# Chunks 10 and 11 of the FFN move to the seven-product second layer, and the order of the whole program is written anew

## The chip, the cores and the metric

The kernel runs on one core of a Trainium2 chip. The metric is the device time of one execution in microseconds (us). Engines: PE is TensorE (matmuls; PEld is its weight load), DVE is VectorE, ACT is ScalarE, POOL is GpSimd, SP is SyncE, which here issues nearly all DMAs. Each engine runs its own instructions strictly in the order in which the program writes them.

## The reference, cut to what matters

```python
# q, k, v: (8, 8, 576, 64); w_ch1: (512, 2048); w_ch2: (2048, 512)
scores = scale * np.matmul(q, k.transpose(0, 1, 3, 2))
mask = (rel >= 0) & (rel < 64)                 # each query sees 64 keys
scores = np.where(mask, scores, -1000000000.0)
scores = scores - np.max(scores, axis=-1, keepdims=True)
attn = np.exp(scores)
attn = attn / (np.sum(attn, axis=-1, keepdims=True) + 1e-09)
x = np.matmul(attn, v)                         # -> (8, 576, 512)
u = x + np.real(np.fft.fft(np.fft.fft(x, axis=1), axis=2))
un = (u - mu) / np.sqrt(var + 1e-06)           # norm over the last axis
out = u + np.maximum(un @ w_ch1, 0.0) @ w_ch2
```

## The kernel before

**Work and tiles.** The 8 x 576 = 4,608 tokens are 36 tiles of 128 tokens, 9 for each pair of batches. Nearly every product is done in fp16 parts: an operand is split into a high and a low half, and a product is three matmuls (`PASSES`: high x high, high x low, low x high).

**Attention, tile by tile.** q, k and v are loaded (L538), from tile 11 on split into halves and turned by transposing DMAs (L593). The PE makes the scores (L662), the DVE masks them and takes the maximum (L677), ACT does the exponential (L685), ACT, POOL and DVE split the result into `flex` (L506, L510, L516), a transposing DMA for each half tile writes it to `pt` (L715), and the PE multiplies by the values, `pa<-ve,pt` and `pa<-va,pt` (L739). The DVE normalises (L758), and another transposing DMA turns the result (L865) for the FFT (L1023, L1061 on the PE). For tiles from 14 on the attention result goes out to DRAM and comes back later (L791, L1228). After a batch's FFT each tile is gathered, normalised and turned by one more transposing DMA, `room<-up` (L1221); `room` then holds the input of the FFN.

**FFN, chunk by chunk.** The tokens form 18 chunks (0 to 17) of 256. The first layer is the same in all: 16 hidden blocks f, each 12 matmuls of 128x128 weights by 256 columns into `ph` (L1419, or L1573 in the newer form). The second layer has two forms.

- `ffn(c)`, for chunks below `SEVEN`: for each f six matmuls of 512 columns, `po<-ws,hh` (L1400); the hidden values are made by ACT (L1428) and DVE (L1431), 512 columns at a time.
- `ffn7(c)`, for chunks from `SEVEN` on: hidden blocks j and j+8 are taken together as a 2x2 block product, done with seven products of sums in place of eight. For each of 8 j there are 7 x 3 = 21 matmuls of 256 columns (L1548). The sums of the hidden values are made by DVE or POOL (L1589), then split (L506, L510, L1597). The sums of the weights, the same for all chunks, are made once by `weight_sums(j)` on the DVE (tiles `td`, L1493 to L1521) and are kept in buffers that attention uses until its end: `flex`, `qbd`, `kst`, `va`, `ve`.

**What sets the order.** The program first lists some 3,000 operations with what each reads and writes. A table of their numbers, `ORDER`, then says in which order they are issued, and a set, `SECOND`, which operations go to their second choice of engine. The FFN chunks are spread under the attention of later tiles, so that the PE has matmuls while DVE, ACT, POOL and the DMAs prepare the next tile. Before the first FFN work, `warm` matmuls (L1759) stand in gaps of the PE. The lines around the change:

```python
            for c in range(max(PLAIN, made), min(SEVEN, ready)):
                ffn(c)
    ...
    for j in range(HALF):
        weight_sums(j, 4000 + 10 * j)
    for c in range(SEVEN, NCH):
        plan.slack = FSLACK
        ffn7(c)
    ...
        for o, gap in zip(plan.follow(ORDER, SECOND), plan.gaps):
```

Of the kernel before, what the change touches and what calls it, by code (L numbers as in the profile page):

```python
# [58 lines left out]
SEVEN = 12  # L59
# [339 lines left out]
def attn_fft_ffn_kernel(ctx: ExitStack, tc: tile.TileContext, q, k, v, w1, w2, gidx, dft_d, dft_s, mask, out):  # L399
# [1311 lines left out]
    for T in range(NTT):  # L1711
# [6 lines left out]
        if n in (4, 8):  # L1718
            base += FFT_AT + (FFT1 if T == 8 else 0)
            fft(2 * pb + n // 8, base)  # L1720
            for i, m in enumerate(range(0, 4) if n == 4 else range(4, 9)):
                args = NT * pb + m, base + NORM_AT + i + (EARLY if T == 4 and i > 1 else 0)
                if args[0] // 2 >= SEVEN + 4:
                    behind.setdefault(args[0] // 2, []).append(args)
# [66 lines left out]
```

## Time and profile before

| what | value |
|---|---|
| median of 3 runs | 944.51 us (944.35 to 948.38) |
| profiled execution, whole | 945.16 us |
| its span in the trace | 943.4 us |
| PE busy in the span | 924.2 us (98%) |
| DVE, ACT, POOL busy | 705.3 us (75%), 435.1 us (46%), 441.5 us (47%) |
| granted PE clock | 1.000 over the whole span |
| last PE instruction of attention | about 654 us |

The span is what the profiler saw between first and last instruction; the 1.8 us between 943.4 and 945.16 lie outside it. Busy times of different engines overlap. A PE that is busy all the time is bound by what it streams; then a DVE that idles costs nothing.

### The profile page before, as it was taken

To read this page: it belongs to the slowest core of one execution; us is meant where nothing else is said; L and a number is where in the kernel's file an instruction comes from. 1 tells how busy PE (TensorE), PEld (TensorE's weight loads), DVE (VectorE), ACT (ScalarE), POOL (GpSimd) and SP (SyncE) were. 2 spreads that over 40 slices of the span, in tenths; PEclk is the share of its full clock that TensorE was granted. 3 is DMA by queue.
4 is the path that set the end of the run, shared out by engine and by line. 5 is a ranking of instruction groups with operands and counts; after the bars stand their busy time and mean duration, and the time that the engine had idled before them with its cause. 6 is when DMAs were issued, how large, how long until landed. Compare 5 with 4: busy or idle time off the path is not lost.

```text
span 943.4 us, 24809 instructions
## 1 busy us (share of the span) xinstructions
PE 924.2 (98%) x9717; PEld 703.2 (75%) x9717; DVE 705.3 (75%) x1982; ACT 435.1 (46%) x979; POOL 441.5 (47%) x823
## 2 busy tenths in 40 slices
PE   7799999999999999999999999999999999999998
PEld 6677777666766676666766676667779998888887
DVE  5898998887767866677658757888898965675664
ACT  6875777834555424445443543444334442422111
POOL 2653464744744555465746544655601454124012
PEclk9999999999999999999999999999999999999999
DMA  9997447999689969879979788785402032210100
GB/s 231 239 263 202 133 144 147 167 173 169 136 193 163 198 122 167 185 152 207 197 168 190 150 162 169 163 147 108 137 12 57 24 96 65 68 35 13 57 24 23
DMA packets 300230, 128.69 MB, mean 136 GB/s; under 512 B 277768, under 2 KB 278152, under 8 KB 300112
## 3 DMA queue, kind: packets, MB, share of 16 engines
q1 hardware_dynamic: 297248, 118.06, 59.6%
q0 software_dynamic: 2720, 8.92, 3.3%
q8 instruction: 76, 1.25, 0.6%
q14 instruction: 42, 0.34, 0.1%
q10 hardware_dynamic: 144, 0.13, 0.0%
HBM read 60.76 MB, written 19.94 MB: 86 GB/s over the span
## 4 chain that ended last, share of the span: by engine, by line
PE 83%; DMA 5%; DVE 4%; POOL 3%; SPq 2%; issue 2%; ACT 1%; POOLq 0%; DVEq 0%; ACTq 0%
PE ph L1419 22%; PE po L1400 22%; PE ph L1573 13%; PE po L1548 11%; PE pz L1061 3%; PE pg L1023 3%; PE pa L739 3%; PE psc L662 2%; DMA kn<-in_k 1%; POOL flex L516 1%; DMA ve<-va 1%; DMA qn<-in_q 1%; DMA pt<-flex 1%; SPq L1277 1%; PE py L850 1%
## 5 line engine op out<-in xcount | busy, mean ns | idle before, releaser
L1400 PE MATMUL po<-ws,hh 128*128 128x512 f16 (+1 forms) x1116 | 284.5, 391 | 0.5 <-issue 0.2
L1419 PE MATMUL ph<-room,ws 128*128 128x256 f16 x2112 | 256.1, 273 | 1.8 <-DVE hh L1431 1.8
L1419 PEld LDWEIGHTS <-ws 128*128 128x128 f16 x2112 | 205.3, 98 | 54.1 <-issue 2.8
L1400 PEld LDWEIGHTS <-hh 128*128 128x128 f16 x1056 | 101.1, 98 | 90.0 <-DVE hh L1431 0.7
L1573 PE MATMUL ph<-room,ws 128*128 128x256 f16 x1152 | 136.2, 273 | 0.0
L1573 PEld LDWEIGHTS <-ws 128*128 128x128 f16 x1152 | 112.6, 98 | 13.6
L1428 ACT ACTIVATE hh<-ph 128x512 f16<-128x512 f32 x88 | 52.3, 594 | 120.8 <-PE ph L1419 99.8
L685 ACT ACTIVATE pr<-pr,nm 128x128 f32<-128x128 f32 x288 | 91.2, 393 | 31.5 <-DVE nm L677 31.4
L1431 DVE SCALAR_TENSOR_TENSOR hh<-ph,hh 128x512 f16<-128x512 f32 x88 | 60.4, 686 | 36.6 <-ACT hh L1428 36.5
L1135 POOL DMA_INDIRECT mt<-md,gix x34 | 42.0, 1235 | 96.7 <-DVE mv L1163 81.5
L677 DVE CUSTOM_DVE_ANT_0 pr<-psc,mskb 128x128 f32<-128x128 f32 x288 | 65.0, 287 | 25.9 <-PE psc L662 19.7
L1584 ACT ACTIVATE hx<-ph 128x512 f32<-128x512 f32 x47 | 27.8, 595 | 113.3 <-PE ph L1573 103.7
L1589 DVE TENSOR_TENSOR hx<-hx 128x128 f32<-128x128 f32 x164 | 45.1, 318 | 37.8 <-ACT hx L1584 36.2
L1548 PEld LDWEIGHTS <-hh 128*128 128x128 f16 x658 | 64.4, 98 | 7.6
L1597 POOL TENSOR_TENSOR hl<-hx,hh 128x256 f16<-128x256 f32 (+1 forms) x40 | 28.0, 730 | 77.3 <-DVE hh L510 53.7
L516 POOL TENSOR_TENSOR up<-un,up 128x128 f16<-128x128 f32 x84 | 40.9, 516 | 46.3 <-ACT up L506 38.8
L516 POOL TENSOR_TENSOR flex<-pr,flex 128x128 f16<-128x128 f32 x92 | 42.5, 494 | 36.2 <-ACT flex L506 18.2
L1548 PE MATMUL po<-ws,hh 128*128 128x256 f16 x282 | 51.2, 273 | 0.0
L1597 DVE TENSOR_TENSOR hl<-hx,hh 128x896 f16<-128x896 f32 x37 | 40.4, 1097 | 7.8 <-ACT hh L506 6.5
L752 POOL TENSOR_TENSOR rc<-rc,mone 128x4 f32<-128x4 f32 x29 | 32.5, 1129 | 26.6 <-DVE rc L747 16.8
L739 PE MATMUL pa<-ve,pt 128*64 128x65 f16 (+1 forms) x776 | 37.0, 203 | 2.5 <-ACT ve L506 1.8
L1548 PE MATMUL po<-ws,hl 128*128 128x256 f16 x141 | 38.4, 273 | 0.0
(244 smaller groups left out, 1718.6 us busy)
## 6 DMA issues: line engine op xcount, KB each, us to landing
room<-in_moe_w_ch SPq DMA_DIRECT2D x20, 512.0 KB
flex<-in_moe_w_ch SPq DMA_DIRECT2D x12, 512.0 KB
ve<-va SPq DMA_DIRECT2D x47, 130.0 KB
flex<-in_v SPq DMA_DIRECT2D x22, 256.0 KB
xs<-xu SPq DMA_DIRECT2D x22, 256.0 KB
xv<-xs SPq DMA_DIRECT2D x22, 256.0 KB
out<-xv SPq DMA_DIRECT2D x21, 256.0 KB
md<-mp SPq DMA_DIRECT2D x24, 192.0 KB
```

The costliest lines, as they stand in the source:

```text
L516: eng.tensor_tensor(out=out[:, k : k + w], in0=in0[:, k : k + w], in1=in1[:, k : k + w], op=al)
L677: nc.vector.tensor_tensor_reduce(out=t["pr", g][:, hp], in0=t["ps", g][:, hp], in1=mskb[:, m : m + P], scale=-0.125, scalar=3.0e38, op0=AL ...
L685: nc.scalar.activation(pr, pr, AF.Exp, bias=t["nm", g][:, hp : hp + 1], scale=-1.0)
L739: nc.tensor.matmul(pa[sl, hp], pt[:, sl], v_, start=(x == 0), stop=(x == len(mm) - 1))
L1400: nc.tensor.matmul(t["po"][i], l_, r_, start=(f == 0 and x == 0), stop=(f == NKF - 1 and x == len(mm) - 1))
L1419: nc.tensor.matmul(ph, l_, r_, start=(x == 0), stop=(x == len(mm) - 1))
L1428: nc.scalar.activation(t["hh", j][:, 0], ph, AF.Relu)
L1431: nc.vector.scalar_tensor_tensor(out=hh[:, 1], in0=ph, scalar=0.0, in1=hh[:, 0], op0=ALU.max, op1=ALU.subtract)
L1548: nc.tensor.matmul(t["po", bk][:, x], t["h", j][a][:, slot], right(n, j, b_), start=(j == 0 and k == 0 and n in opens), stop=(j == seven - ...
L1573: nc.tensor.matmul(ph, l_, r_, start=(x == 0), stop=(x == len(mm) - 1))
L1589: eng.tensor_tensor(out=x[:, o], in0=x[:, p0], in1=x[:, p1], op=al)
L1597: eng.tensor_tensor(out=lo[:, a:b_], in0=x[:, a + 1 : b_ + 1], in1=hi[:, a:b_], op=ALU.subtract)
```

## The change

`SEVEN` goes from 12 to 10: chunks 10 and 11 leave `ffn` for `ffn7`. The seven-product form then has eight chunks, 10 to 17. The two-layer chunks 0 to 9 alone are left for the time before and during attention. `ORDER` and `SECOND` are written anew for the whole program. Nothing else in the code differs.

```diff
-SEVEN = 12
+SEVEN = 10
 AWAY = 14
 
 ORDER = [int(i) for i in """
-1 115 0 9 7 116 3 15 118 119 120 145 121 124 144 129 16 149 125 130 173 126 131 147 150 117 127 148 17 132 21 18 176 153
...
+8 0 9 3 7 116 14 115 15 120 121 144 145 118 119 124 125 126 127 129 130 149 150 117 123 16 146 173 147 148 131 122 128
...
```

Counted over the program on the PE: 192 fewer matmuls of 512 columns at L1400 and 336 more of 256 columns at L1548; 384 matmuls of the first layer change their line from L1419 to L1573; 48 `warm` matmuls in place of 45. On the other engines: the four-part sums of L1589 go from 164 to 196 on the DVE and from 24 to 56 on POOL; L1597 from 37 to 47 on the DVE and from 40 to 64 on POOL; L1431 on the DVE from 88 to 72.

Fewer chunks now lie under attention. Between the scores of tile 20 and those of tile 32 the PE had 81 groups of L1419 (12 matmuls) and 81 of L1400 (6 matmuls); now 61 and 62. The transfers that load q, k and v or transpose (1,024 packets of at most 256 bytes each) between these two places are 109 before and 103 now. Between the scores of tile 26 and of tile 32 the groups go from 39 and 39 to 30 and 31, and the transfers from 55 to 56.

First place, the PE at the second half of tile 31's product with the values (`pa<-ve,pt` and `pa<-va,pt`). `pt_0` and `pt_1` are the two buffers that the turned halves take in turn. Before, 36 matmuls of L1400, 83 of L1419 and 24 of L1023 stand between the tile's scores and this place:

```order
L1419 LDWEIGHTS ws
L1419 MATMUL ph_4_9579<-room,ws 128x256
L1419 LDWEIGHTS ws
L1419 MATMUL ph_4_9579<-room,ws 128x256
L739 LDWEIGHTS pt_0_9516
L739 MATMUL pa_0_9602<-ve_85,pt_0_9516 64x65
L739 LDWEIGHTS pt_0_9516
L739 MATMUL pa_0_9602<-va_83,pt_0_9516 64x65
```

and of the kernel changed, where 18 matmuls of L1400, 36 of L1419, 12 of L1061 and 48 of L739 stand between:

```order
L1400 LDWEIGHTS hh_6_8717
L1400 MATMUL po_1_8148<-ws,hh_6_8717 128x512
L1400 LDWEIGHTS hh_6_8717
L1400 MATMUL po_1_8148<-ws,hh_6_8717 128x512
L739 LDWEIGHTS pt_1_8926
L739 MATMUL pa_1_8996<-ve_85,pt_1_8926 64x65
L739 LDWEIGHTS pt_1_8926
L739 MATMUL pa_1_8996<-va_83,pt_1_8926 64x65
```

The same product now stands closer behind the scores of its own tile.

Second place, the queue of SP around the transposes that make these `pt` tiles (`room` is the FFN's input, `qbd`, `kst`, `va`, `ve` are parts of q, k and v, `md` goes to DRAM, `py` is a turned result for the FFT). Before:

```order
L1221 DMA_TRANSPOSE room<-up_9447 128x8x128
L715 DMA_TRANSPOSE pt_1_9489<-flex 128x8x128
L715 DMA_TRANSPOSE pt_0_9516<-flex 128x8x128
L538 DMA qbd_79<-in_q 128x8x64
L624 DMA ve_85<-va_83 64x520
L538 DMA flex<-in_v 128x8x64
L1086 DMA md_7577<-mp_2_9184 96x512
L865 DMA_TRANSPOSE py_9654<-yp_9542 128x8x128
```

and of the kernel changed:

```order
L593 DMA_TRANSPOSE qbd_78<-flex 128x8x128
L593 DMA_TRANSPOSE kst<-flex 128x8x128
L715 DMA_TRANSPOSE pt_1_8926<-flex 128x8x128
L1086 DMA md_7626<-mp_1_8899 96x512
L1221 DMA_TRANSPOSE room<-up_8870 128x8x128
L538 DMA flex<-in_v 128x8x64
L1228 DMA xv_8974<-xs_7128 128x512
L715 DMA_TRANSPOSE pt_0_9023<-flex 128x8x128
```

The transpose of `pt_1` now stands right behind the two that turn the next tile's q and k.

Third place, the DVE at the first weight sums (`td`). `ws` holds the weights. Before, with the work on tile 34 around them:

```order
L1194 TENSOR_SCALAR un_10182<-xv_9949,rs_10198,nb_10364 128x512
L1431 SCALAR_TENSOR_TENSOR hh_1_10224<-ph_1_10133,hh_1_10224 128x512
L516 TENSOR_TENSOR yT_9166<-yT_9166 128x4x96
L1493 TENSOR_TENSOR td_0_10400<-ws 128x512
L1493 TENSOR_TENSOR td_0_10400<-td_0_10400,ws 128x512 x2
L1500 TENSOR_TENSOR td_1_10401<-ws,td_0_10400 128x256
L1501 TENSOR_TENSOR td_1_10401<-td_1_10401,ws 128x256
L1502 TENSOR_TENSOR td_1_10401<-ws,td_1_10401 128x256
```

and of the kernel changed:

```order
L1431 SCALAR_TENSOR_TENSOR hh_6_9810<-ph_6_9699,hh_6_9810 128x512
L955 SCALAR_TENSOR_TENSOR h_6_9917<-h_6_9692,yT_8587 128x388
L1493 TENSOR_TENSOR td_0_9919<-ws 128x512
L1493 TENSOR_TENSOR td_0_9919<-td_0_9919,ws 128x512 x2
L1500 TENSOR_TENSOR td_1_9920<-ws,td_0_9919 128x256
L1501 TENSOR_TENSOR td_1_9920<-td_1_9920,ws 128x256
L1502 TENSOR_TENSOR td_1_9920<-ws,td_1_9920 128x256
L1503 TENSOR_TENSOR td_1_9920<-td_1_9920,ws 128x256
```

From the first of these rows to the last `td` row the DVE has 246 instructions before and 220 in the kernel changed. The whole of attention moves likewise: the last tile's scores stood on the PE inside chunk 10, and stand now at the start of chunk 9.

## Rows read from the trace of the kernel before

**Rows 1.** The page: busy time by engine, and slices of the span.

```profile
PE 924.2 (98%) x9717; PEld 703.2 (75%) x9717; DVE 705.3 (75%) x1982; ACT 435.1 (46%) x979; POOL 441.5 (47%) x823
...
PEclk9999999999999999999999999999999999999999
DMA  9997447999689969879979788785402032210100
```

**Rows 2.** Windows: busy time by engine in four stretches.

```profile
core 0: us, PE busy (x) PEld busy (x) DVE busy (x) ACT busy (x) POOL busy (x), PEclk, DMA share, GB/s
0.00:23.60 23.60, 18.64 (x244) 14.53 (x244) 11.99 (x64) 14.86 (x37) 7.00 (x23) 1.00 0.97 231
23.60:60.00 36.40, 30.66 (x407) 24.54 (x406) 33.10 (x118) 28.98 (x76) 26.04 (x41) 1.00 0.99 242
190.00:640.00 450.00, 445.83 (x5282) 315.27 (x5281) 327.31 (x1021) 201.62 (x497) 246.95 (x494) 1.00 0.87 169
790.00:840.00 50.00, 50.00 (x460) 44.81 (x459) 35.29 (x87) 18.31 (x29) 15.37 (x26) 1.00 0.23 59
```

**Rows 3.** The chain of waits, 396 to 425 and 800 to 815 us.

```profile
398.08 1.29 PE po L1400 x6
399.37 1.31 PE ph L1419 x12
...
803.51 2.29 PE po L1548 x21
805.81 1.31 PE ph L1573 x12
```

**Rows 4.** Groups of instructions by line, shapes apart (busy us, mean ns).

```profile
L1400 PE MATMUL po<-ws,hh 128*128 128x512 f16 x1056 | 256.4, 379 | 0.5 <-issue 0.2 <-DVE hh L1431 0.2
...
L1548 PEld LDWEIGHTS <-hh 128*128 128x128 f16 x658 | 64.4, 98 | 7.6
L1431 DVE SCALAR_TENSOR_TENSOR hh<-ph,hh 128x512 f16<-128x512 f32 x88 | 60.4, 686 | 36.6 <-ACT hh L1428 36.5
...
L1589 DVE TENSOR_TENSOR hx<-hx 128x128 f32<-128x128 f32 x164 | 45.1, 318 | 37.8 <-ACT hx L1584 36.2
```

**Rows 5.** What the PE waited for, 150 to 943 us (total, times, longest).

```profile
PE ph L1419 <- DVE hh L1431: 1.8, 3, 1.3
PE psc L662 <- issue: 1.3, 3, 0.6
PE pa L739 <- DMA ve<-va: 0.5, 1, 0.5
```

**Rows 6.** DMA packets, 195 to 245, 275 to 325 and 240 to 640 us.

```profile
DMA packets 30779, 9.16 MB, mean 183 GB/s; under 512 B 30068, under 2 KB 30068, under 8 KB 30772
...
DMA packets 29114, 9.35 MB, mean 187 GB/s; under 512 B 28191, under 2 KB 28191, under 8 KB 29108
...
DMA packets 183852, 67.48 MB, mean 169 GB/s; under 512 B 173231, under 2 KB 173231, under 8 KB 183795
```

**Rows 7.** Windows: three stretches with the DMA engines fullest.

```profile
195.00:245.00 50.00, 50.00 (x534) 35.01 (x533) 40.69 (x123) 23.05 (x56) 22.03 (x39) 1.00 0.98 183
275.00:325.00 50.00, 49.28 (x588) 33.62 (x586) 36.66 (x129) 26.55 (x61) 23.86 (x45) 1.00 0.99 187
440.00:490.00 50.00, 49.82 (x655) 36.62 (x653) 31.83 (x110) 24.97 (x65) 32.52 (x68) 1.00 0.97 186
```

**Rows 8.** Timeline of tile 33: scores, transpose issue, product with the values.

```profile
596.59 0.86 PE L662 MATMUL psc<-kst,qbd 64*64 64x128 f16 x48
...
604.50 2.61 SPq L715 DMA_TRANSPOSE pt<-flex  x2
...
610.47 0.22 PE L739 MATMUL pa<-ve,pt 128*64 128x65 f16 x1
```

**Rows 9.** Windows: the stretch of the weight sums.

```profile
615.00:738.00 123.00, 123.00 (x1146) 93.97 (x1145) 108.12 (x255) 48.20 (x100) 46.02 (x85) 1.00 0.39 87
```

276 rows, old and new, of tables (ORDER, SECOND) are left out of this document.

## The prediction

> **What bounds the kernel.** I read the page first. The PE is busy for 98% of the span, and its granted clock is full in all 40 slices [rows 1]. The kernel is bound by what the PE streams. Then come windows: where does the PE idle at all? In the first 60 us it idles 4.96 + 5.74 us with the DMA engines at 97 to 99%; in the 450 us from 190 to 640 it idles 4.17 us; from 790 on, where only seven-product chunks run, it idles nowhere in 50 us [rows 2]. The sum of idle time over the span is 943.4 - 924.2 = 19.2 us [rows 1], so more than half of it is the prologue. What little the PE waits for in the middle and the end names a hidden value not ready and one late transfer, and no single wait is above 1.3 us [rows 5]. So there are two questions: how many us of matmuls go away, and whether the PE stays fed when attention's work lies closer together.
>
> **What the second layer saves.** The chain shows both forms running without a gap. Six matmuls of 512 columns take 1.29 us, and the 21 matmuls of 256 columns take 2.29 us [rows 3]. A chunk has 16 groups of the first (20.64 us) or 8 of the second (18.32 us). That is 2.32 us less a chunk and 4.64 us for chunks 10 and 11. The first layer costs 1.31 us per 12 matmuls in both [rows 3], so its change of line is worth nothing. 1.29/6 = 215 ns and 2.29/21 = 109 ns: the per-matmul spacing gives 96 x 215 - 168 x 109 = 2.33 us, the same. I take -4.7 us with rounding; the rows leave no more than 0.1 either way. The 512-column matmul's mean of 379 ns [rows 4] is an end-to-end duration of a pipelined instruction, and must not be multiplied.
>
> The weight loads rise: 144 more of them, 98 ns each [rows 4]. They lie beside matmuls of 109 ns, and the stretch from 790 to 840 runs with PEld busy 44.81 of 50 and the PE without a gap [rows 2]. I cost them at nothing. Without that cover they would cost up to 144 x 98 ns = 14 us, but the same loads at the same spacing are hidden there already.
>
> A rule speaks against this. The rows show 215 ns between 512-column matmuls and 109 ns between 256-column ones [rows 3]. The Trainium skill, in TensorE: Matmul & The Clock Gate, section Back-to-back issue gap, gives a sustained spacing of about 131 ns for a 512-column and 81 ns for a 128-column matmul in a stream of weight loads and matmuls; an estimate for 256 columns between those two figures is some 98 ns. By that rule the second layer would go from 96 x 131 ns = 12.6 us to 168 x 98 ns = 16.5 us a chunk, a loss of 3.9 us, where the rows give a gain of 2.3 us. The trace does not agree with that rule; it agrees with the page's other formula, which it keeps for isolated matmuls (N/2.4 + 2.5 ns, about 216 and 109 ns). Whoever drops this paragraph loses no term of the sum.
>
> The extra sums on ACT, DVE and POOL for chunks 10 and 11 are those of the pure stretch, where the DVE is busy 35.29 of 50 us and the PE waits for nothing [rows 2]. They trade 16 of the 686 ns instructions of L1431 for 32 four-part sums on the DVE at 318 ns each [rows 4], and the rest on POOL. Nothing.
>
> **What drawing attention together costs.** Two chunks fewer lie under attention, so the same preparation must be done in less PE time. Pricing the counted groups by 1.31 and 1.29 us [rows 3] and the other PE work (attention, FFT) at about 43 us before and 40 after, the stretch from tile 20's scores to tile 32's falls from 81 x 2.60 + 43 = 254 us to 61 x 1.31 + 62 x 1.29 + 40 = 200 us. The tightest half, from tile 26 to tile 32, falls from 39 x 2.60 + 22 = 123 us to 30 x 1.31 + 31 x 1.29 + 21 = 100 us, with 55 transfers before and 56 after. (The 43, 22 and 21 are counted rows of the order at this trace's durations, good to 1 us.)
>
> *DMA.* A transfer here is 1,024 short packets. From 240 to 640 us the DMA engines moved 173,231 of these, 0.423 transfers a us, at 87% busy over most of it [rows 2, 6]. From 195 to 245 and 275 to 325 us they moved 30,068 and 28,191, which is 0.587 and 0.551 a us, at 98 and 99% [rows 6, 7]. The new table asks for 103/200 = 0.515 over the long stretch and 56/100 = 0.56 in the half. That lies between the two best rates seen, so the DMA engines will be full for some 100 us. Bounds: at 0.587 they do it in 95.4 us and cost nothing; at 0.551 they need 101.6 us, 1.6 us more; no row shows what a lower rate would be in such a mix, and at the mean of rows 6's long stretch, 0.423, it would be 132 us, 32 us more, but that mean is a demand and not a limit. In the fullest windows of before the PE lost 0.00, 0.72 and 0.18 us in 50 [rows 7], so a full DMA does not by itself stop the PE. I take the worse of the two full rates, +1.6 us.
>
> *The short lead.* Tile 31 after the change has 18 matmuls of L1400, 36 of L1419, 12 of L1061 and 48 of L739 between its scores and its last product: 3.9 + 3.9 + 1.3 + 0.9 = 10.0 us, and 10.9 with the 0.86 us of the scores [rows 8]. Mask, exponential, split and transpose must fit in there. The shortest lead in the trace of before is tile 33's, 610.47 - 596.59 = 13.9 us without a stall [rows 8]; there the transpose was issued at 604.50, 7.9 us after the scores, and so 6.0 us passed until the use. So between 0 and 3 us can be missing. If it is late, the scores of tile 32 and the next FFN group on the PE are late behind it, and with them the next masked scores. This place lies in the same half, so I do not add it to the 1.6 us.
>
> *The weight sums.* They use the DVE while attention ends. Before, from 615 to 738 us, the DVE was busy 108.12 of 123 us (88%) and the PE idled nowhere [rows 9]. At that window's 0.424 us an instruction the 220 instructions of after take 93 us, in about 113 us of PE work: 83%. Bounds 0 and +3 us; I take 0.
>
> *The prologue.* Its 10.7 us of idle time [rows 2] is set by loads: the DMA engines are full, and the new order asks for about the same bytes before each step. It can move 2 us either way; I take 0.
>
> **Sum.** 945.16 (this profiled execution: the 943.4 span and 1.8 outside) - 4.7 + 1.6 = 942.1. That execution lies 0.65 us above the median of 944.51, so the forecast against the median is **941.4 us**. 0.5% is 4.7 us, about what a measurement of this kernel can tell from no change: faster is below 939.8, slower above 949.2. The bare saving ends just on the line between faster and same.
>
> **Rivals.**
> - *All is hidden, or the new table closes gaps.* The PE lost 4.2 us from 190 to 640 and 10.7 us in the prologue [rows 2]; a new order of everything may win some of it back. Then 944.5 - 4.7 - (0 to 4) = 936 to 939.8. For it: full DMA windows that cost nothing [rows 7]. Against: the same DMA-bound prologue.
> - *The gain is eaten.* The short lead and the weight sums each lose their 3 us, or the DMA rate is 0.53 in the tight half (56/0.53 = 105.7, +5.7 us): 943 to 949.2.
> - *Slower: the DMA engines cannot hold the rate.* One place, from tile 26 to 32, and one price: 56 transfers at rate r take 56/r. At 0.535 the saving is gone; at 0.512 (109.4 us, +9.4) it is slower; at 0.50 the added 12 us give 951.8. For it: only those two windows show such rates, for 50 us each, and the queue of SP is in order, so that one late transpose holds all behind it. Against: both windows did hold it.
> - *The spacing rule.* If 512-column matmuls streamed at a spacing below that of rows 3 elsewhere, the change would add matmul time, 952 us by the page's figures above. The chain speaks against it.
>
> **Chances.** Forecast (939.8 to 942.8) 0.37; all hidden or better 0.36; eaten (942.8 to 949.2) 0.11; DMA slower 0.15; spacing rule 0.01. So faster 0.36, same 0.48, slower 0.16. Range: the forecast's own is 939.8 to 942.8; 8 in 10 must reach over the gains and into the slower case, 936.5 to 951.0, leaving out about 0.06 below and 0.11 above.
>
> **What would show it.** Right: groups of six at 1.29 us and of 21 at 2.29 us for chunks 10 and 11; DMA share at 97 to 99% for some 100 us before attention ends, with under 3 us of PE idle there; attention's end some 60 us earlier, at about 590 us; an idle PE nowhere after it. Wrong: waits of L739 or L662 on `pt` or on loads of several us each between tiles 26 and 32 (slower), waits of L1548 on `td`'s products at the first seven-product chunk (eaten), or a prologue whose idle time falls far below 10.7 us (better).

## The result, and the profile after

The change made the kernel slower: 956.71 us (median of 8 runs, 951.07 to 959.55) against 944.16 us for the kernel before (8 runs, 941.09 to 948.38). The ratio is 1.0128, with a 95% interval of 1.0103 to 1.0154. The forecast was 941.4 us in a range up to 951.0, so the time lies outside the range: slower, where a small gain or no change was forecast. The profiled execution took 957.04 us, with a span of 955.3 us, 11.9 us above the span before.

The page of the kernel after answers to [rows 1]. The PE is busy as before, 923.6 us, though 4.7 us of matmuls are gone; the clock of the next rows answers for most of that. The span is longer, and the DMA line now reads 9 in eleven slices of 24 us in a row.

```profile
PE 923.6 (97%) x9864; PEld 719.7 (75%) x9864; DVE 711.4 (74%) x1986; ACT 454.1 (48%) x1015; POOL 487.1 (51%) x897
...
PEclk9999999999999999999999999999999999999999
DMA  9966566999799999999999895520121130111110
```

Windows of the kernel after, by stretch; the first two and the next two answer to [rows 2], and the last four run from the scores of tile 15 to those of 20, on to 26, to 32 and to 35. Columns as in [rows 2]: for each engine the busy time, then granted PE clock, DMA share and GB/s.

```profile
0.00:23.60 23.60, 18.92 (x222) 14.78 (x222) 10.77 (x50) 11.88 (x29) 5.83 (x22) 0.95 0.95 223
23.60:60.00 36.40, 30.22 (x418) 25.12 (x415) 31.85 (x121) 28.40 (x76) 24.11 (x35) 0.94 0.95 231
...
190.00:640.00 450.00, 434.50 (x5244) 308.43 (x5242) 348.48 (x1065) 222.56 (x547) 296.22 (x576) 1.00 0.94 176
790.00:840.00 50.00, 50.00 (x460) 44.82 (x459) 28.32 (x63) 15.72 (x25) 17.73 (x30) 1.00 0.13 33
...
227.30:313.80 86.50, 81.83 (x1036) 58.16 (x1035) 65.39 (x212) 42.42 (x107) 57.29 (x111) 1.00 0.97 176
313.80:418.00 104.20, 101.28 (x1269) 71.46 (x1268) 83.67 (x254) 50.15 (x127) 67.94 (x129) 1.00 1.03 188
418.00:524.20 106.20, 100.85 (x1290) 71.75 (x1288) 79.76 (x257) 55.37 (x138) 68.03 (x140) 1.00 1.10 206
524.20:576.30 52.10, 50.73 (x604) 35.40 (x598) 38.36 (x121) 27.44 (x67) 42.30 (x86) 1.00 0.88 168
```

The same four stretches of the kernel before, between the scores of the same tiles:

```profile
222.90:317.20 94.30, 93.58 (x1128) 66.53 (x1120) 69.10 (x223) 48.58 (x119) 50.01 (x104) 1.00 0.86 168
317.20:450.60 133.40, 131.77 (x1512) 93.47 (x1510) 93.50 (x278) 55.44 (x134) 76.95 (x150) 1.00 0.86 171
450.60:575.30 124.70, 123.95 (x1479) 88.08 (x1478) 85.14 (x272) 55.98 (x142) 69.17 (x155) 1.00 0.89 169
575.30:624.50 49.20, 49.20 (x558) 33.86 (x554) 40.10 (x122) 21.09 (x52) 29.00 (x52) 1.00 0.81 166
```

Read the second number of each row against the first. Between tiles 15 and 35 the PE idled 4.67 + 2.92 + 5.35 + 1.37 = 14.3 us after, and 0.72 + 1.63 + 0.75 + 0 = 3.1 us before: 11.2 us more. Tile 15's scores stood at 222.9 us before and at 227.3 after: 4.4 us more. Most of this is the PE's clock and not idle time: the first two rows have a granted clock of 0.95 over 23.6 us and 0.94 over 36.4 us, which is 3.4 us of full-speed time lost, where [rows 2] have 1.00; the PE's idle time in these 60 us is 10.9 us after and 10.7 before. Against that stand the 4.7 us of the second layer. 11.2 + 4.4 - 4.7 = 10.9 of the 11.9 us; most of the rest is 0.7 us of idle time between 570 and 680 us, where the kernel before had none [rows 9].

What the PE waited for from 150 to 943 us after (total, times, longest), which answers to [rows 5]: two transposes now lead the list, and no DMA but one value load was there before.

```profile
PE pa L739 <- DMA pt<-flex: 7.0, 5, 2.7
PE ph L1419 <- DVE hh L1431: 2.6, 4, 0.8
PE psc L662 <- DMA kst<-flex: 2.2, 2, 1.7
PE py L850 <- DVE y L516: 1.7, 3, 0.8
PE pa L739 <- DVE nm L677: 1.6, 1, 1.6
```

DMA packets between the scores of tiles 20 and 32, first before (317.2 to 575.3 us):

```profile
DMA packets 121879, 43.94 MB, mean 170 GB/s; under 512 B 115120, under 2 KB 115120, under 8 KB 121842
```

and after (313.8 to 524.2 us), with what its transposes of `pt` took from issue to landing (last number, median us):

```profile
DMA packets 114872, 41.49 MB, mean 197 GB/s; under 512 B 108471, under 2 KB 108471, under 8 KB 114841
...
pt<-flex SPq DMA_TRANSPOSE x25, 4.3
```

115,120 / 1,024 / 258.1 us is 0.436 transfers a us; 108,471 / 1,024 / 210.4 us is 0.503. The table had asked for 0.515 over this stretch and 0.56 in its second half. The packets make some 3% more than the transfers counted in the table (105.9 for 103), so by that count the stretch ran at 103 / 210.4 = 0.490 and its second half at 56 / 106.2 = 0.527. The DMA share there is 1.03 and 1.10: the packets' times add up to more than 16 engines' time. A share above 1 means that such times overlap, so it does not tell by itself how full the engines are.

### The profile page after: what moved, and what is told of

It is laid out like the page before. It is cut to its first block, busy times and chain, and to the rows that moved or that the text cites. A ratio compares the mean times of both kernels' runs of the same rounds, so it can differ in the third digit from the quotient of the medians.

```text
span 955.3 us, 25289 instructions
## 1 busy us (share of the span) xinstructions
PE 923.6 (97%) x9864; PEld 719.7 (75%) x9864; DVE 711.4 (74%) x1986; ACT 454.1 (48%) x1015; POOL 487.1 (51%) x897
## 4 chain that ended last, share of the span: by engine, by line
PE 70%; DMA 12%; DVE 7%; POOL 6%; issue 2%; SPq 2%; ACT 2%; DVEq 0%; POOLq 0%; ACTq 0%
PE ph L1573 18%; PE po L1548 15%; PE po L1400 14%; PE ph L1419 13%; DMA pt<-flex 4%; PE pa L739 2%; PE pg L1023 2%; PE pz L1061 2%; DMA py<-yp 2%; DMA room<-up 2%; PE psc L662 2%; POOL rc L752 1%; DVE y L516 1%; DVE pr L677 1%; DMA flex<-in_v 1%
## 5 line engine op out<-in xcount | busy, mean ns | idle before, releaser
L1400 PE MATMUL po<-ws,hh 128*128 128x512 f16 (+1 forms) x924 | 238.1, 394 | 0.0
L1419 PE MATMUL ph<-room,ws 128*128 128x256 f16 x1728 | 209.5, 273 | 2.8 <-DVE hh L1431 2.6
L1419 PEld LDWEIGHTS <-ws 128*128 128x128 f16 x1728 | 167.7, 98 | 43.8 <-issue 4.7
L1573 PE MATMUL ph<-room,ws 128*128 128x256 f16 x1536 | 180.4, 273 | 0.0
L1573 PEld LDWEIGHTS <-ws 128*128 128x128 f16 x1536 | 150.3, 98 | 18.0
L1400 PEld LDWEIGHTS <-hh 128*128 128x128 f16 x864 | 81.9, 98 | 73.2 <-DVE hh L1431 0.4
L1548 PEld LDWEIGHTS <-hh 128*128 128x128 f16 x882 | 86.2, 98 | 10.0
L1428 ACT ACTIVATE hh<-ph 128x512 f16<-128x512 f32 x72 | 42.8, 595 | 82.8 <-PE ph L1419 70.1
L1589 POOL TENSOR_TENSOR hx<-hx 128x128 f32<-128x128 f32 x56 | 27.9, 519 | 102.3 <-ACT hx L1584 60.9
L1589 DVE TENSOR_TENSOR hx<-hx 128x128 f32<-128x128 f32 x196 | 53.2, 313 | 35.5 <-ACT hx L1584 33.7
L1548 PE MATMUL po<-ws,hh 128*128 128x256 f16 x378 | 68.6, 273 | 0.0
L1597 DVE TENSOR_TENSOR hl<-hx,hh 128x896 f16<-128x896 f32 x47 | 51.5, 1096 | 22.6 <-ACT hh L506 21.4
L1597 POOL TENSOR_TENSOR hl<-hx,hh 128x256 f16<-128x256 f32 x64 | 41.9, 687 | 48.0 <-DVE hh L510 27.3
L1431 DVE SCALAR_TENSOR_TENSOR hh<-ph,hh 128x512 f16<-128x512 f32 x72 | 49.2, 684 | 18.9 <-ACT hh L1428 18.7
L506 ACT CAST hh<-hx 128x896 f16<-128x896 f32 x39 | 36.4, 938 | 53.3 <-DVE hx L1589 41.2
L516 POOL TENSOR_TENSOR y<-xu 128x128 f32<-128x128 f32 x68 | 38.7, 600 | 29.0 <-DVE xu L758 21.2
L1176 POOL TENSOR_SCALAR rs<-mv 128x1 f32<-128x1 f32 x36 | 13.6, 376 | 76.3 <-ACT un L1170 74.7
```

Of the source, the lines that this page charges most:

```text
L516: eng.tensor_tensor(out=out[:, k : k + w], in0=in0[:, k : k + w], in1=in1[:, k : k + w], op=al)
L1400: nc.tensor.matmul(t["po"][i], l_, r_, start=(f == 0 and x == 0), stop=(f == NKF - 1 and x == len(mm) - 1))
L1419: nc.tensor.matmul(ph, l_, r_, start=(x == 0), stop=(x == len(mm) - 1))
L1428: nc.scalar.activation(t["hh", j][:, 0], ph, AF.Relu)
L1431: nc.vector.scalar_tensor_tensor(out=hh[:, 1], in0=ph, scalar=0.0, in1=hh[:, 0], op0=ALU.max, op1=ALU.subtract)
L1548: nc.tensor.matmul(t["po", bk][:, x], t["h", j][a][:, slot], right(n, j, b_), start=(j == 0 and k == 0 and n in opens), stop=(j == seven - ...
```

## The experiments

Ratios are against the kernel before, timed beside each. In all, four theories stood against each other: the DMA engines' rate (A), the short leads on the engines (B), the prologue, and the table as such.

### The start alone, both ways

The first 850 operations (to about tile 14) are the same set in both tables but for seven on either side, so the tables can be spliced. The engine choices in `SECOND` go with the operations.

```diff
-ORDER = after
+ORDER = before[:850] + [i for i in after if i not in before[:850]]
```

> The changed kernel, with the first 850 operations of its table in the order of the table before (up to about tile 14; the rest as changed). If the new order of the prologue costs the 4.4 us by which tile 15's scores came later (222.9 to 227.3 us), this takes 952 to 953 us and those scores stand near 223 us. If the prologue's loss is made good later anyway, because the DMA engines set the pace from 250 us on, it stays within 1.5 us of 956.7.

> The kernel before, with the first 850 operations in the order of the new table. If the new prologue costs 4 us by itself, 948 us; if it costs something only together with the drawn-together attention, 944 us.

The old start in the changed kernel: 956.28 us, ratio 1.0134 (1.0116 to 1.0153). Nothing is won. The old start does bring tile 15's scores to 223.4 us, but those of tile 20 come at 313.4, as in the changed kernel (313.8): the 4 us are given back within five tiles, to one wait above all:

```profile
PE ph L1425 <- DVE hh L1437: 4.1, 1, 4.1
```

(L1437 here is L1431 of the kernel before: a hidden value made by the DVE.) The new start in the kernel before: 949.51 us, ratio 1.0050 (1.0032 to 1.0068), with runs from 945.16 to 954.02 and one at 960.12, so by itself it does cost some 5 us. The profiled execution is the fastest of these, with tile 15's scores at 223.7 us and full clock up to there, and so it does not show where the 5 us lie. Over the eleven runs up to 954.02 us the share of the clock that was not granted is 2.3 us a run on average, against 0.9 us for the kernel before beside them; that is some 1.4 of the 5 us. The prologue was a loss of the new table, but not one that adds up with the other: whatever comes earlier to tile 15 waits there.

### Fewer packets, and less work on the engines

```diff
-                nc.sync.dma_start(t[nm][o : o + m], ap)
+                if T >= 15:
+                    bb, s0 = divmod(P * n + o, S)
+                    ap = src[b0 + bb].rearrange("h (a c) d -> (h a) c d", c=8)[s0 : s0 + m]
+                nc.sync.dma_start(t[nm][o : o + m], ap)
```

> The changed kernel, whose loads of q, k and v from tile 15 on take the same bytes in rows of 2,048 bytes in place of 256 (the values then stand in other places, which changes the result and no instruction of the engines). Theory A, the DMA engines cannot hold the packet rate that the new table asks for: the PE's idle time from 200 to 650 us falls from 15.5 us to 6 or less and the time to 945 to 949 us. Theory B, the short leads between scores and product leave too little time for DVE, ACT and POOL: the idle time stays at 13 to 16 us and the time at 954 to 957 us.

```diff
-                copy(eng, t["pp", g][:, :, 0], t["pr", g])
+                k = 4 if T < 15 else 1
+                copy(eng, t["pp", g][:, 0:k, 0], t["pr", g][:, 0:k])
...
-                    copy(eng, two[:, 0], t[nm].rearrange("p h d -> p (h d)"))
+                    w = 512 if T < 15 else 128
+                    copy(eng, two[:, 0, 0:w], t[nm].rearrange("p h d -> p (h d)")[:, 0:w])
```

(and the same cut for the low halves)

> The changed kernel, whose splits of q, k and of the exponentials from tile 15 on are made for a quarter of the columns (the rest keeps values of an earlier tile); every transfer stays. It takes some 1.2 us of ACT, DVE and POOL work off each chain from scores to product. Theory B (the chain on the engines is too long): idle time from 200 to 650 us at 6 us or less, 945 to 949 us. Theory A (the DMA engines): 13 to 16 us idle, 954 to 957 us.

Long packets: 950.15 us, ratio 1.0058 (1.0040 to 1.0077), 6.5 us off the changed kernel. Light splits: 952.58 us, ratio 1.0071 (1.0046 to 1.0096), 4.1 us off. Each theory had asked for a cure by its own edit and none by the other's, and both fell short: each edit cured a part. The windows from 200 to 650 us, changed kernel, long packets and light splits in turn:

```profile
200.00:650.00 450.00, 434.50 (x5207) 311.03 (x5206) 349.75 (x1056) 220.45 (x539) 290.49 (x566) 1.00 0.92 174
```

```profile
200.00:650.00 450.00, 439.21 (x5252) 315.68 (x5251) 355.66 (x1065) 221.91 (x542) 290.75 (x566) 1.00 0.84 174
```

```profile
200.00:650.00 450.00, 440.88 (x5233) 315.55 (x5231) 324.67 (x1058) 200.70 (x541) 235.98 (x515) 0.99 0.91 174
```

15.5 us of idle PE became 10.8 and 9.1. In the first edit the DMA share fell (0.92 to 0.84), in the second the DVE's and POOL's work (by 25 and 55 us); the transfers were the same, and the DMA share stayed at 0.91.

### The rate alone, in the kernel before

```diff
+            if o.idx in extra:
+                n = extra.index(o.idx)
+                more = dr.tile([P, H, D], F32, tag=f"more{n}", name=f"more{n}", bufs=1)
+                nc.sync.dma_start(more, q[n % 8, :, P * (n // 8) : P * (n // 8) + P].rearrange("h s d -> s h d"))
```

> The kernel before, with 22 more transfers of 1,024 packets of 256 bytes (from the input to DRAM that nobody reads), one behind each fifth of the 109 between the scores of tiles 20 and 32: 131 in 254 us of PE work, 0.515 a us, the rate that the new table asks for. Theory A (the DMA engines do not hold that rate): the PE falls behind by 5 to 10 us there, 949 to 954 us. Theory B (what stalls is the short lead, and this kernel's leads are long): 944 to 946 us.

955.32 us, ratio 1.0122 (1.0095 to 1.0150). This kernel has the old table, the old leads and the old matmuls, and 22 transfers more cost it as much as the whole change. Its windows between the scores of tiles 20, 26 and 32, and its packets from tile 20 to 32:

```profile
315.70:454.90 139.20, 134.19 (x1507) 94.04 (x1502) 92.88 (x278) 55.28 (x134) 74.30 (x147) 0.99 0.95 179
454.90:584.40 129.50, 125.91 (x1475) 89.37 (x1474) 86.61 (x272) 56.04 (x142) 71.41 (x158) 0.99 0.94 191
```

```profile
DMA packets 144426, 49.62 MB, mean 185 GB/s; under 512 B 137676, under 2 KB 137676, under 8 KB 144388
```

137,676 / 1,024 / 268.7 us is 0.500 a us, near the 0.503 of the changed kernel, which has another order and other leads and asks for the same 0.515. That does not make 0.50 a limit. Both are transfers divided by the time that the stretch took, so any stall lowers them, and in this run the two halves differ:

```profile
DMA packets 70458, 24.88 MB, mean 179 GB/s; under 512 B 66827, under 2 KB 66827, under 8 KB 70440
...
DMA packets 73968, 24.74 MB, mean 191 GB/s; under 512 B 70849, under 2 KB 70849, under 8 KB 73948
```

These are 0.469 a us over 139.2 us and 0.534 over 129.5 us, with 5.0 and 3.6 us of idle PE. What is shown is the price of the transfers: 22 more of them cost this kernel 11 us. Theory B alone would have left it at 944 to 946 us; it falls as a full account.

One rival goes untested. The added transfers also take their turn in the queue of SP, which issues them in order. By its instructions' own times in the traces SP spent 169 of 258.1 us on issuing DMAs between these tiles in the kernel before, 174 of 210.4 us in the changed one and 194 of 268.7 us here; with long packets it was 155 of 207.0 us. No run separates the DMA engines from this queue, so "transfers" stands for both below.

### Both reliefs, and their control

Both edits together, in the changed kernel, then with the old start, then in the kernel before.

> The changed kernel with long packets and light splits together. The two took 6.5 and 4.1 us apart. If they cure different waits, the sum: 946 us and some 8 us of PE stall left between the scores of tiles 15 and 35, of 18.9; if they cure the same ones, 949 to 950 us; if the two theories together are all of it, 943 us.

> The kernel with both reliefs and the table's first 850 operations in the old order. With the DMA engines relieved the 4 us that the old start brings (tile 15's scores at 223 and not 227 us) should no longer be given back by tile 20: 4 us below the run with both reliefs. If they are given back all the same, no difference, and it is not the DMA engines that set the pace from tile 15 to 20.

> The control of the run with both reliefs: the kernel before (six seven-product chunks, its own table) with the same long packets and light splits from tile 15 on. If its own attention holds without them, it stays at 943 to 945 us, and the changed kernel with both reliefs (943.1 us) has lost its 4.7 us elsewhere (its prologue, 3 us); if the reliefs take time off the kernel before too, 940 to 942 us, and what they took off the changed kernel was in part no matter of the change.

| kernel with both edits | us | ratio to the kernel before |
|---|---|---|
| changed | 943.07 | 0.9990 (0.9974 to 1.0006) |
| changed, old start | 943.59 | 1.0006 (0.9985 to 1.0026) |
| before | 942.45 (beside 945.45) | 0.9972 (0.9957 to 0.9986) |

On the changed kernel the two take off 13.6 us, more than 6.5 + 4.1; on the kernel before 0.28%, 2.6 us. So about 11 us of the changed kernel's loss depend on the transfers and on the splits that feed them, close to the 11.2 us of idle time read above. With that gone the two kernels stand 1.7 us apart (0.9990 to 0.9972), with intervals that overlap. The 4.7 us are still not seen. The profiled executions say where some of it is: from 200 to 650 us the PE idled 4.7 us in the first, 5.4 in the second, 1.4 in the third,

```profile
200.00:650.00 450.00, 445.33 (x5316) 321.69 (x5315) 333.60 (x1075) 205.17 (x549) 235.65 (x515) 1.00 0.84 173
```

```profile
200.00:650.00 450.00, 444.59 (x5340) 322.19 (x5339) 338.68 (x1094) 202.94 (x548) 231.21 (x504) 1.00 0.81 173
```

```profile
200.00:650.00 450.00, 448.65 (x5275) 318.31 (x5274) 303.70 (x1023) 182.27 (x498) 198.31 (x443) 1.00 0.79 168
```

and tile 15's scores stood at 228.0, 223.0 and 221.7 us. The old start did come earlier by 5 us in the profiled execution, but the medians of the first two are the same. By the expectation, then, it is not the DMA engines that set the pace from tile 15 to 20. The profile of the second names one wait there, again for a hidden value from the DVE, right behind tile 15's scores:

```profile
PE ph L1432 <- DVE hh L1444: 3.2, 1, 3.2
```

Where the rest went stays open.

### Later products, and other tables

```diff
-... 2230 ...            # a product with the values that stalled 1.5 us
+... one or two FFN groups, 2230 ...
```

> The changed kernel, whose table puts one or two of the next FFN groups ahead of ten of the PE's attention operations that stalled between 227 and 608 us (13 groups, 16.9 us of matmuls, ahead of 11.0 us of stall; nothing else moves). Theory B (the leads are a little too short): most of those 11 us come back, 946 to 949 us. Theory A (the DMA engines set the pace whatever stands between): the stalls come back at later places, 954 to 957 us.

953.69 us, ratio 1.0116 (1.0081 to 1.0152): 3.0 us less by the medians and 1.1 us by the ratios, whose intervals overlap, so it is not clear of noise; neither theory's number, nearer to A. The idle time from 200 to 650 us went from 15.5 to 10.6, and new stalls came up where FFN groups now stand earlier, one of 1.8 us on a hidden value from the DVE; the largest, 2.9 us on a `pt`, had found no group to go ahead of it and stayed.

The last three have tables found by a search that prices attention's transfers 10 to 16% higher than the kernel's own cost list.

> Eight seven-product chunks as in the change, and a third table, found by a search that prices each transfer of attention 10 to 16% above the 1.45 to 1.5 us of the kernel's own cost list and leaves the PE some slack. Between the scores of tiles 20 and 32 it asks for 97 transfers beside 65 groups of L1419 and 64 of L1400 (some 208 us, 0.467 a us; the change 0.515), between 26 and 32 for 45 in some 102 us (0.44; the change 0.56). If the loss lies in how evenly the table loads the DMA engines, the 4.7 us of matmuls come through: 938 to 943 us. If it lies in there being two chunks fewer under attention, whatever the table, 949 us or more.

> Seven seven-product chunks (11 to 17): half the step of the change, with a table of the same search: 105 transfers beside 69 and 70 groups between the scores of tiles 20 and 32 (some 222 us, 0.47 a us). Half the saving is 2.3 us: 941 to 944 us if the table holds; between the two others if the number of chunks decides.

> The control: the kernel before, six seven-product chunks, with a table of the same search. It tells what the search is worth by itself. If the table before loses little (the PE idled 4.2 us from 190 to 640 us and 10.7 in the prologue), 941 to 945 us.

| seven-product chunks | us | ratio | idle PE, 200 to 650 us |
|---|---|---|---|
| 6 (12 to 17) | 945.12 | 1.0012 (0.9995 to 1.0029) | 0.9 |
| 7 (11 to 17) | 948.25 | 1.0041 (1.0021 to 1.0061) | 3.2 |
| 8 (10 to 17) | 951.98 | 1.0075 (1.0045 to 1.0105) | 9.7 |

The search is worth nothing at six chunks, and at eight it takes 4.7 us off the change's own table. But each chunk more makes the kernel slower, by 3.1 and 3.7 us, though its matmuls save 2.3. The idle times are of single executions (944.11, 945.42 and 954.04 us), of which the last was the slowest of its seven and the other two were among the fastest of theirs, so they overstate the difference. The eight-chunk table asked for 0.467 and 0.44 transfers a us, and its largest stalls wait on other things (3.8 us of an FFT product on the DVE, 2.2 on a hidden value). By packets, between the scores of tiles 20 and 32, it ran at 0.482 a us with 7.7 us of idle PE; the seven-chunk table ran at 0.485 with 0.7. The mean rate alone does not tell which table stalls. Evening out the transfers does not bring the 4.7 us through; that expectation fell. No version here that computes the same values is faster than the kernel before.

## Why the prediction was wrong

**What bounds the kernel, and the saving: right.** The chain of the kernel after shows chunks of the new form in the same time as before, which answers to [rows 3], with no gap between these groups:

```profile
691.85 2.29 PE po L1548 x21
694.14 2.62 PE ph L1573 x24
696.76 2.29 PE po L1548 x21
699.05 2.62 PE ph L1573 x24
```

21 matmuls in 2.29 us are 109 ns each. By the Trainium skill (TensorE: Matmul & The Clock Gate, Back-to-back issue gap) 512-column matmuls would stand at 131 ns and these, by an estimate between its figures for 128 and 512 columns, at 98 ns. This trace again does not agree (six of 512 columns take 1.29 us, 215 ns each, in the chain below), so the loss is not that rule's. The weight sums and the extra sums for chunks 10 and 11 cost under 1 us, as forecast: from 570 to 680 us the PE was busy 109.31 of 110.

**The short lead: right that little was at stake, wrong in the row.** Tile 31's second product, the lead of 10.9 us, did not wait at all; what waited 1.4 us right behind tile 31's scores was the product of tile 30, whose transpose took 6.29 us to land. The chain there:

```profile
507.25 6.29 DMA pt<-flex
513.54 0.04 issue
513.59 0.95 PE pa L739 x48
...
519.88 1.29 PE po L1400 x6
```

**The step that failed** is "I take the worse of the two full rates, +1.6 us", the term for what drawing attention together costs. It priced that cost as a rate of the DMA engines, in the half from tile 26 to 32 alone, and let everything else hide. Measured, the PE idled 11.2 us more than before, and in all of tiles 15 to 32 (4.67, 2.92 and 5.35 us). Two windows of 50 us [rows 6, 7] had given 0.587 and 0.551 transfers a us, and I took them for rates at which the PE stays fed for 100 us and more; in the kernel with more transfers, 0.534 a us over 129.5 us came with 3.6 us of idle PE. Nor was the rate the whole of it: lighter splits, which leave every transfer as it is, took idle time away too (15.5 to 9.1 us), and long packets and light splits together took 13.6 us off. The chain from a tile's scores to its product, transfers and splits in turn, is what no longer fitted, as far as these runs show.

The rival "the DMA engines cannot hold the rate" was the nearest: it named 951.8 us and had 0.15. It had a part of the cause, and its price was charged to one half of the stretch. That it came within 5 us is in part luck, since it left out the splits and the next term.

**A second term was mis-sized:** the prologue, "I take 0" within 2 us, came out 4.4 us late at tile 15. I had looked at its idle time alone, and that did hold (10.9 us against 10.7). What I had put at nothing without a reason is the PE's clock: 3.4 us of full-speed time went there in the profiled execution. Over all eight runs the share of the clock that was not granted is 4.2 us a run, against 0.9 us in the seventeen runs of the kernel before beside the first experiments, so some 3 of the 12.5 us are clock. The two splices show that the new start costs time by itself (5 us in the kernel before), and that the loss did not add to this result.

**What stays open.** The reliefs show that the loss hangs on transfers and splits together, and the added transfers show that more transfers alone suffice to cause such a loss. Whether they do so in the DMA engines or in the queue of SP is not shown, nor whether transfers land later when the engines are full: the median from issue to landing of the `pt` transposes between the scores of tiles 20 and 32 was 4.3 us in the changed kernel and 4.2 us with both edits, where the stalls are nearly gone. Why an even table still loses 9.7 us with eight chunks is not settled. Its DVE is about as busy as the change's (354.68 and 349.75 of 450 us), and its stalls name the DVE, DMA and ACT; that two chunks fewer leave too little PE work to cover attention's chains, whichever of them is late, is argued here and not shown.

The Trainium skill (DMA: Bandwidth & Descriptors, Why small descriptors are slow) gives a fixed overhead of 3 cycles in 11 for a packet of 256 bytes. By that, an estimate, rows of 2,048 bytes save about 24% of a load. The run with long packets agrees in size: its hardware queue used 91.9% of 207.0 us in place of 100.9% of 210.4 us, 22 us less over some 37 loads. That is 0.6 us each, of about 2 us that a transfer takes on average (212 us over 106).

## What to carry to other kernels

A rate read from the fullest window does not tell that the PE stays fed at that rate for longer: before work is packed closer, add transfers to the kernel as it is and see what they cost. Work that hides other work has a price of its own: a matmul taken away under attention is worth its time only if the attention can be drawn together by as much. The granted clock belongs in the sum beside busy and idle time. And a gain or loss ahead of a stretch that is paced by something else is lost or made good there, so a splice of the two orders tells more than the sum of the parts.

## What the runs showed of the hardware

A PE that idled for some us got a lower clock right after in some places of these runs, and not in others. In the run with the old start the PE was busy 0.88 us of 5, and in the next 5 us its granted clock averaged 0.75, a mix of the two levels of 2.4 and 1.2 GHz (first two rows below). In the kernel after, 3.12 of 5 us busy in the prologue were followed by 0.66. In the run with both edits and the old start, 1.79 of 5 us were followed by full clock (last two rows):

```profile
225.00:230.00 5.00, 0.88 (x6) 0.32 (x4) 3.72 (x9) 2.17 (x5) 5.00 (x9) 0.91 0.63 123
230.00:235.00 5.00, 5.00 (x30) 3.43 (x29) 4.90 (x19) 3.09 (x10) 2.60 (x6) 0.75 1.04 138
```

```profile
15.00:20.00 5.00, 3.12 (x37) 2.46 (x36) 4.80 (x22) 3.65 (x11) 0.15 (x1) 1.00 1.05 256
20.00:25.00 5.00, 4.76 (x69) 3.90 (x69) 3.13 (x18) 2.66 (x8) 4.11 (x7) 0.66 1.10 304
```

```profile
225.00:230.00 5.00, 1.79 (x15) 1.31 (x14) 4.97 (x23) 3.10 (x9) 4.30 (x11) 1.00 0.47 91
230.00:235.00 5.00, 5.00 (x36) 3.38 (x35) 4.86 (x10) 2.01 (x7) 2.19 (x5) 1.00 1.02 170
```

At 0.66 over 5 us, 1.7 us of full-speed time are lost on top of the stall. The kernel before had full clock throughout, though it idled 10.7 us in its first 60 us [rows 2], so idle time alone does not tell when this price falls due. I had not counted it at all.
